# A gated linear-attention kernel: the key-value sums on two 64-column TensorE tiles, and an earlier load of the second x tile

## The chip, the cores and the metric

The kernel runs on one core of a Trainium2 chip. The metric is the device time of one execution in microseconds (us): 257.1 us before the change, the median of three runs (256.88 to 257.52). One profiled execution of the same kernel, from which every line of a profile below is taken, had a span of 255.7 us from its first to its last instruction.

The engines are TensorE (PE, matrix products; PEld is its loading of weights), VectorE (DVE), ScalarE (ACT), GpSimd (POOL) and SyncE (SP), whose queue issues most of the transfers. [...]

## What is computed

One block of 2048 tokens by 1024 features. Two branches share the input `x`, and a gate mixes them. Cut to what matters here:

```python
def reference(A_x, A_wqkv, A_wo, B_x, B_w_r, B_w_gate, B_w_up, B_w_down, gate_w):
    def _A_ref(x, wqkv, wo):
        B, S, D = x.shape
        H = 32; Dh = D // H                       # 32 heads of 32
        qkv = (x @ wqkv).reshape(B, S, 3, H, Dh).transpose(2, 0, 3, 1, 4)
        q, k, v = qkv[0], qkv[1], qkv[2]
        phi = lambda t: jnp.where(t > 0, t + 1, jnp.exp(t)) + 1e-6
        pq, pk = phi(q), phi(k)
        kv = jnp.einsum("bhsd,bhse->bhde", pk, v)  # 32 x 32 per head
        z = jnp.einsum("bhsd->bhd", pk)            # column sums of pk
        num = jnp.einsum("bhqd,bhde->bhqe", pq, kv)
        den = jnp.einsum("bhqd,bhd->bhq", pq, z)[..., None] + 1e-6
        return (num / den).transpose(0, 2, 1, 3).reshape(B, S, D) @ wo
    # _B_ref: one token, the one with the largest x @ w_r, gets a gated
    # feed-forward update; all others pass x through
    g = sigmoid((x * gate_w).sum(-1, keepdims=True))
    return g * a + (1 - g) * b
```

The part that changes is `kv` and `z`: a product over all 2048 tokens of the 32 columns of `pk` of a head with the 32 columns of `v` of the same head, and the sum of each `pk` column.

## The kernel before

The 2048 tokens are 16 tiles of 128. For each token tile, TensorE makes K and V (`unit_KV`; 8 matmuls for each 512 output columns), ScalarE and VectorE apply phi to K and write it to `pk`, and ScalarE copies V to `vt`. `unit_KVACC` then adds the tile's share to `kv`. It takes eight groups of 128 columns (four heads each). In each, `pk` is the stationary operand and `vt`, with a column of ones behind its 128 columns, the moving one. The result is 128 x 129: four useful 32 x 32 blocks on the diagonal, the products of different heads beside them, which nobody reads, and the column sums as column 128. The accumulators stay in three PSUM banks until the last token tile is done.

```python
def kv_slot(g):
    return kvacc[g // 3][:, 129 * (g % 3) : 129 * (g % 3) + 129]

def kv_open(t):
    if t not in pk_t:
        pk_t[t] = kvp.tile([P, D], BF, tag="pk", name=f"pk{t}")
        vt_t[t] = kvp.tile([P, NG, 129], BF, tag="vt", name=f"vt{t}")
        nc.gpsimd.memset(vt_t[t][:, :, 128:129], 1.0)

def unit_KVACC(t):
    for g in range(NG):
        pe.matmul(kv_slot(g), lhsT=pk_t[t][:, g * P : (g + 1) * P], rhs=vt_t[t][:, g, :],
                         start=False, stop=False, skip_group_check=True)
    del pk_t[t], vt_t[t]
```

The main loop puts this block of work between the K and V matmuls of the next token tile, beside the query matmuls (`unit_Q`) and pieces of the feed-forward branch (`ffn_step`; its matmuls use four 32-column tiles of TensorE side by side, as do the router logits `rps`, the denominators `dps` and the final sum `yps`):

```python
# ... rps: the router and gate logits of all tokens ...
for t in range(4):
    unit_KVACC(t)
for t in range(4, NT):
    for nb in range(4):
        unit_KV(t, nb)
        if nb == 1 and t > 4:
            unit_KVACC(t - 1)
        if (t, nb) in GU_AFTER:
            ffn_step(4)
        # ... steps of the down projection, on VectorE ...
    # ... unit_Q, once or twice per t; more ffn_step at the end of some t ...
unit_Q(*q_units.popleft())
unit_KVACC(NT - 1)
down_finish()          # yps
```

At the start, the first two token tiles of x are loaded as they are and transposed on TensorE (`unit_T`), and the rows of the K weights are used in the order in which they arrive:

```python
load_x(0, 1)           # all on SyncE's queue, in this order
load_k(0)
load_k(1)
load_x(1, 1)
for c in range(2, KC):
    load_k(c)
# ...
unit_T(0)
warm(3, 128)
first_mm(0, 0, 2)      # token tile 0, K rows 0 and 1
unit_T(1)
for c in range(2, KC):
    first_mm(0, c, c + 1)
    if c < KC - 1:
        first_mm(1, c - 2, c - 1)
first_mm(1, 5, 6)
es = [phi_exp(first[0][nb][:]) for nb in range(2)]
first_mm(1, 6, 8)
```

At the end, each token tile's output is made in two halves of 512 columns. The last half of the last token tile is cut in two, so that the last eviction and the last transfer are short.

Of the kernel before, what the change touches and what calls it, by code (L numbers as in the profile page):

```python
# [13 lines left out]
BF = mybir.dt.bfloat16  # L14
F32 = mybir.dt.float32
# [7 lines left out]
P = 128  # L23
# [3 lines left out]
NT = S // P  # L27
KC = D // P
NG = D // P
# [12 lines left out]
def kernel(  # L42
# [13 lines left out]
    nc = tc.nc  # L56
# [6 lines left out]
    keep = ctx.enter_context(tc.tile_pool(name="keep", bufs=1))  # L63
# [9 lines left out]
    def in_order(engine, names):  # L73
        last = [None]

        def wrap(fn):
            def call(*a, **k):
                inst = fn(*a, **k)  # L78
                if last[0] is not None and strict[0]:
                    tc.add_manual_dep(inst.ins, last[0].ins.name, NOSYNC, reason="program order on this engine")  # L80
                last[0] = inst
                return inst

            return call

        return SimpleNamespace(**{n: wrap(getattr(engine, n)) for n in names})

    pe = in_order(nc.tensor, ["matmul", "transpose"])
    dve = in_order(nc.vector, ["memset", "tensor_copy", "tensor_scalar", "tensor_scalar_add", "tensor_tensor", "scalar_tensor_tensor",
                               "reciprocal", "max", "max_index", "tensor_reduce", "stream_shuffle"])  # L90
    sp = in_order(nc.sync, ["dma_start", "dma_start_transpose"])
    act = in_order(nc.scalar, ["activation", "copy"])
# [1 line left out]
    pq_all = keep.tile([P, NG, S], BF)  # L94
    gate = keep.tile([P, NT], F32)
    omg = keep.tile([P, NT], F32)
    kvbd = keep.tile([P, NG, P], BF)
    zc = keep.tile([P, NG, 32], BF)
    mzc = keep.tile([P, NG, 32], F32)
    xp = dram.tile([S, D], BF, name="xp")  # L100
# [7 lines left out]
    kvp = ph1.enter_context(tc.tile_pool(name="kvp", bufs=4))  # L108
# [11 lines left out]
    def load_x(t0, n):  # L120
        xt4 = xin.tile([P, n, D], BF, name=f"xnat{t0}", bufs=1)
        sp.dma_start(out=xt4[:, 0:n, :], in_=x_v[:, t0 : t0 + n, :])
        for i in range(n):
            xnat[t0 + i] = xt4[:, i, :]

    def load_k(c):
        sp.dma_start(out=wkv[:, c, 0:D], in_=wqkv_v[:, c, D : 2 * D])

    load_x(0, 1)
    load_k(0)  # L130
    load_k(1)
    load_x(1, 1)
    for c in range(2, KC):
        load_k(c)
    for t in (2, 3):
        sp.dma_start_transpose(out=xT[:, :, t * P : (t + 1) * P], in_=x2d[t * P : (t + 1) * P, :])
# [37 lines left out]
    kvacc = []  # L174

    def kv_slot(g):
        return kvacc[g // 3][:, 129 * (g % 3) : 129 * (g % 3) + 129]

    def phi_exp(ps):
        u = tmp.tile([P, 512], F32, tag="phi_u")  # L180
# [5 lines left out]
    def phi_dve(ps, e0, out_ap):  # L186
        dve.scalar_tensor_tensor(out_ap, ps, EPS, e0[:], op0=ALU.max, op1=ALU.add)
# [11 lines left out]
    pk_t = {}  # L199
    vt_t = {}  # L200

    def kv_open(t):
        if t not in pk_t:
            pk_t[t] = kvp.tile([P, D], BF, tag="pk", name=f"pk{t}")
            vt_t[t] = kvp.tile([P, NG, 129], BF, tag="vt", name=f"vt{t}")
            nc.gpsimd.memset(vt_t[t][:, :, 128:129], 1.0)  # L206

    def kv_mm(ps, t, nb, c0, c1):
        for c in range(c0, c1):
# [3 lines left out]
    def kv_evac(ps, t, nb):  # L213
        if nb < 2:
            phi_dve(ps[:], phi_exp(ps[:]), pk_t[t][:, 512 * nb : 512 * nb + 512])
        else:
            act.copy(vt_t[t][:, 4 * (nb - 2) : 4 * (nb - 2) + 4, 0:128], ps[:].rearrange("p (g e) -> p g e", g=4))

    def unit_KV(t, nb):
        kv_open(t)  # L220
# [3 lines left out]

    def unit_KVACC(t):
        for g in range(NG):
            pe.matmul(kv_slot(g), lhsT=pk_t[t][:, g * P : (g + 1) * P], rhs=vt_t[t][:, g, :],
                             start=False, stop=False, skip_group_check=True)
        del pk_t[t], vt_t[t]

    def unit_Q(g, j):
        ps = ps_work.tile([P, 512], F32, tag="w")
        for c in range(KC):
            pe.matmul(ps[:], lhsT=wq[:, c, g * P : (g + 1) * P], rhs=xT[:, c, 512 * j : 512 * j + 512],
                             start=(c == 0), stop=(c == KC - 1))
        phi_evac(ps[:], pq_all[:, g, 512 * j : 512 * j + 512])
# [15 lines left out]
    def first_mm(t, c0, c1):  # L252
        for c in range(c0, c1):
            for nb in range(2):
                kv_mm(first[t][nb], t, nb, c, c + 1)

    unit_T(0)
    warm(3, 128)
    first_mm(0, 0, 2)
    unit_T(1)  # L260
    for c in range(2, KC):
        first_mm(0, c, c + 1)
        if c < KC - 1:
            first_mm(1, c - 2, c - 1)
    first_mm(1, 5, 6)
    es = [phi_exp(first[0][nb][:]) for nb in range(2)]
    first_mm(1, 6, 8)
    for nb in range(2):
# [3 lines left out]
    for t in (2, 3):  # L272
        kv_open(t)
        for nb in range(2):
            pool, tag = (ps_t, "t") if t == 2 else (ps_work, "w")
            ps = pool.tile([P, 512], F32, tag=tag)
# [1 line left out]
            kv_evac(ps, t, nb)  # L278
    ps_t_cm.__exit__(None, None, None)
    ps_acc = ph1.enter_context(tc.tile_pool(name="ps_acc", bufs=1, space=PSUM))  # L280
    kvacc += [ps_acc.tile([P, 512], F32, name=f"kvacc{i}") for i in range(3)]
    off16 = const.tile([P, 1], F32)
    dve.tensor_copy(off16[:], off16_i[:])
    for a in kvacc:
# [11 lines left out]
    for c in range(KC):  # L296
        for j in range(4):
            pe.matmul(rps[32 * j : 32 * j + 32, :], lhsT=wrg_pad[:, c, :], rhs=xT[:, c, 512 * j : 512 * j + 512],
                                  start=(c == 0), stop=(c == KC - 1), tile_position=(0, 32 * j))
# [219 lines left out]
    for t in range(4):  # L519
        unit_KVACC(t)  # L520
    for t in range(4, NT):
        for nb in range(4):
            unit_KV(t, nb)
            if nb == 1 and t > 4:
                unit_KVACC(t - 1)
            if (t, nb) in GU_AFTER:
                ffn_step(4)
            steps = DOWN_STEPS.get(t, ())
            if nb < len(steps):
                down_step(steps[nb])  # L530
        for i in range(Q_PER_T[t]):
            unit_Q(*q_units.popleft())
            if 4 + i < len(steps):
                down_step(steps[4 + i])
            if t == 4 and i == 0:
                router_part1()
                ffn_prefetch()
        if t == 5:
            router_part2()
        if (t, "end") in GU_AFTER:  # L540
            ffn_step(4)
    unit_Q(*q_units.popleft())
    unit_KVACC(NT - 1)
    down_finish()
    gates()
# [1 line left out]
    unit_Q(*q_units.popleft())  # L547

    zcol = keep.tile([P, NG], F32)
    for i in range(3):  # L550
        n = 3 if i < 2 else 2
        acc3 = kvacc[i][:, 0 : 129 * n].rearrange("p (g e) -> p g e", e=129)
        dve.tensor_copy(zcol[:, 3 * i : 3 * i + n], acc3[:, :, 128])
    dve.tensor_tensor(zc[:], mzc[:], zcol[:].unsqueeze(2).to_broadcast([P, NG, 32]), op=ALU.mult)
    for i in range(3):
        n = 3 if i < 2 else 2
        acc3 = kvacc[i][:, 0 : 129 * n].rearrange("p (g e) -> p g e", e=129)
        dve.tensor_copy(kvbd[:, 3 * i : 3 * i + n, :], acc3[:, :, 0:128])
    ph1.close()

    pb = ctx.enter_context(tc.tile_pool(name="pb", bufs=1))
# [51 lines left out]
    def unit_kvT():  # L613
        pt = four_banks("pt")
        for hf in range(2):
            for r in range(4):
                for c in range(4):
                    pe.matmul(pt[c][32 * r : 32 * r + 32, 32 * hf : 32 * hf + 32],
                              lhsT=kvbd[32 * c : 32 * c + 32, 4 * hf + r, 32 * c : 32 * c + 32],
                              rhs=ident[32 * c : 32 * c + 32, 32 * c : 32 * c + 32],  # L620
                              start=True, stop=True, tile_position=(32 * c, 32 * r))
        for c in range(4):
            eng = dve.tensor_copy if c % 2 else act.copy
            eng(kvT[:, :, c, :], pt[c][:, 0:64].rearrange("p (h d) -> p h d", h=2))
# [28 lines left out]
    for t in range(NT):  # L653
        xt = fin.tile([P, D], BF, tag="x3")
        nc.sync.dma_start(out=xt[:], in_=xp[t * P : (t + 1) * P, :])
        xg = fin.tile([P, D], F32, tag="xg3")
        strict[0] = True
        act.activation(xg[:], xt[:], ACTF.Copy, scale=omg[:, t : t + 1])
        strict[0] = False
        ot = fin.tile([P, D], BF, tag="o3")  # L660
        cols = [(0, 512), (512, 512)] if t < NT - 1 else [(0, 512), (512, 256), (768, 256)]
        for c0, cw in cols:
            ps = ps_work.tile([P, 512], F32, tag="w")
            for g in range(NG):
                pe.matmul(ps[:, 0:cw], lhsT=pq_all[:, g, t * P : (t + 1) * P], rhs=m_sb[:, g, c0 : c0 + cw],
                                 start=(g == 0), stop=(g == NG - 1))
            dve.scalar_tensor_tensor(ot[:, c0 : c0 + cw], ps[:, 0:cw], gate[:, t : t + 1],
                                           xg[:, c0 : c0 + cw], op0=ALU.mult, op1=ALU.add)
            if t == NT - 1:
                nc.sync.dma_start(out=out2d[t * P : (t + 1) * P, c0 : c0 + cw], in_=ot[:, c0 : c0 + cw])  # L670
        if t < NT - 1:
            nc.sync.dma_start(out=out2d[t * P : (t + 1) * P, :], in_=ot[:])
        if t == 0:
            rdB = den_group(1)
            normalise(rdB, 2)
            normalise(rdB, 3)
        norm_step(NORM_PER_T[t])
# [30 lines left out]
```

## The time and the profile before

| | value |
|---|---|
| time, median of 3 | 257.1 us (256.88 to 257.52) |
| span of the profiled execution | 255.7 us |
| busy: TensorE, VectorE, ScalarE, GpSimd | 97%, 58%, 49%, 18% |
| granted TensorE clock | 0.999 |
| K, V, Q and output matmuls of 512 columns, start to start | 0.216 us |
| 128 kv matmuls of 129 columns | 221 ns each as recorded |
| start of the first full-width K matmul; start of the unbroken stretch | 4.7 us; 8.4 us |
| last eviction | 483 ns, from 251.9 us |

How to read it. A matmul is recorded with its start and an end that is modelled. Matmuls follow each other much faster than the recorded length of one, so what a matmul costs the queue is the distance from its start to the next one's start. In the timeline, a line is a stretch of like instructions: start, length, engine, line of the program, operation, output and inputs, the part of the array in use (rows\*columns: 128\*32 is one of four column tiles), the shape, and how many. In brackets stands how long the engine was idle before and what ended that. The chain of waits goes back from the last instruction to what released each step, and gives the share of each engine in it.

### The profile page before, as it was taken

Reading aid. Unit: us, or ns where it says so; the run is one execution under the profiler, and the core shown is the slowest. Engines: PE = TensorE matmul, PEld = TensorE weight load, DVE = VectorE, ACT = ScalarE, POOL = GpSimd, SP = SyncE. Lnnn points to the kernel's source line nnn. Section 1 sums busy time; section 2 is a strip of 40 time slices with the busy share of each in tenths; the row PEclk is TensorE's granted clock in tenths of the full one; section 3 lists DMA queues with packets and bytes.
Section 4 is the critical chain, followed back from the end, with each engine's and each line's share of the span. In section 5 each row is a group of like instructions: output and inputs, shape, how many; then the busy total and the mean of one; then the engine's idle time right before and its main releaser. Section 6 shows DMA issues by size and latency. Waiting matters only on the chain.

```text
span 255.7 us, 3936 instructions
## 1 busy us (share of the span) xinstructions
PE 247.7 (97%) x1471; PEld 115.1 (45%) x1498; DVE 147.8 (58%) x243; ACT 125.7 (49%) x200; POOL 47.0 (18%) x94
## 2 busy tenths in 40 slices
PE   7899999999999999999999999999999999999993
PEld 3444455445444444445444444444444444444442
DVE  0046015232246349996799813584888999953442
ACT  2096334556354444645446445468889533333200
POOL 5000001010000000000000000210566779950000
PEclk9999999999999999999999999999999999999999
DMA  6999990009999999878897760030000474454122
GB/s 178 312 336 227 260 329 7 0 19 352 348 341 320 291 275 360 266 229 299 313 489 216 180 151 0 4 123 23 0 1 3 130 223 159 143 187 141 64 82 83
DMA packets 47498, 47.72 MB, mean 187 GB/s; under 512 B 18604, under 2 KB 35380, under 8 KB 47416
## 3 DMA queue, kind: packets, MB, share of 16 engines
q1 hardware_dynamic: 47192, 47.34, 60.6%
q8 instruction: 11, 0.18, 0.3%
q0 software_dynamic: 256, 0.14, 0.2%
q14 instruction: 7, 0.06, 0.1%
q10 hardware_dynamic: 32, 0.00, 0.0%
HBM read 39.34 MB, written 8.40 MB: 187 GB/s over the span
## 4 chain that ended last, share of the span: by engine, by line
PE 95%; DMA 2%; issue 1%; SPq 1%; DVE 0%
PE ps L78 86%; PE kvacc L78 3%; PE first L78 2%; DMA wkv<-in_A_wqkv_dram 2%; PE dps L78 1%; PE rps L78 1%; SPq L78 1%; PE pm L78 1%; PE yps L78 0%; DVE ot L78 0%; PE xs_ps L78 0%; PE hps L78 0%; PE pt L78 0%; PE wps L78 0%
## 5 line engine op out<-in xcount | busy, mean ns | idle before, releaser
L78 PE MATMUL ps<-wkv,xT 128*128 128x512 bf16 x465 | 107.1, 379 | 0.7
L78 PEld LDWEIGHTS <-xT 128*128 128x128 bf16 x512 | 48.8, 98 | 59.1 <-issue 4.5
L78 PE MATMUL ps<-xT,wq 128*128 128x512 bf16 x250 | 57.4, 379 | 0.6 <-issue 0.5
L78 ACT ACTIVATE u<-ps 128x512 f32<-128x512 f32 x60 | 35.9, 598 | 40.4 <-PE ps L78 37.2
L78 PE MATMUL ps<-m_sb,pq_all 128*128 128x512 bf16 (+1 forms) x259 | 55.3, 372 | 0.3
L78 ACT ACTIVATE e<-u 128x512 f32<-128x512 f32 x64 | 40.3, 630 | 2.0
L606 POOL TENSOR_TENSOR pq_all<-pq_all,rb 128x512 bf16<-128x512 bf16 x32 | 36.6, 1169 | 14.4 <-DVE rb L78 14.0
L78 PEld LDWEIGHTS <-pq_all 128*128 128x128 bf16 x264 | 25.8, 98 | 29.8 <-issue 0.4
L78 PEld LDWEIGHTS <-wq 128*128 128x128 bf16 x256 | 24.5, 98 | 30.3 <-issue 1.7
L78 DVE SCALAR_TENSOR_TENSOR pq_all<-ps,e 128x512 bf16<-128x512 f32 x32 | 22.0, 688 | 25.7 <-ACT e L78 25.6
L78 DVE SCALAR_TENSOR_TENSOR yacc<-wt,hcol,yacc 128x1024 f32<-128x1024 bf16 x27 | 34.6, 1281 | 2.2 <-DMA wt<-in_B_w_down_dram 1.7
L78 ACT CAST vt<-ps 128x512 bf16<-128x512 f32 x32 | 18.8, 588 | 34.5 <-PE ps L78 34.5
L78 DVE SCALAR_TENSOR_TENSOR ot<-ps,gate,xg 128x512 bf16<-128x512 f32 (+1 forms) x33 | 24.0, 735 | 15.0 <-PE ps L78 14.0
L78 ACT ACTIVATE xg<-xt,omg 128x1024 f32<-128x1024 bf16 x16 | 18.1, 1146 | 25.8 <-DVE ot L78 25.8
L78 DVE SCALAR_TENSOR_TENSOR pk<-ps,e 128x512 bf16<-128x512 f32 x28 | 19.2, 687 | 19.6 <-ACT e L78 19.6
L78 DVE STREAM_SHUFFLE rb<-rdp 128x512 f32<-128x512 f32 x32 | 22.8, 746 | 0.0
L206 POOL MEMSET vt<- 128x8 bf16 x16 | 1.9, 138 | 108.8 <-PE kvacc L78 108.8
L78 PEld LDWEIGHTS <-pk 128*128 128x128 bf16 x128 | 8.5, 98 | 3.3 <-issue 0.4
L78 PE MATMUL kvacc<-vt,pk 128*128 128x129 bf16 x128 | 9.7, 221 | 0.1
L78 PE MATMUL first<-wkv,xT 128*128 128x512 bf16 x31 | 7.8, 395 | 0.8 <-DMA wkv<-in_A_wqkv_dram 0.6
L78 DVE CAST r_bf<-rps 128x512 bf16<-128x512 f32 x1 | 0.7, 692 | 12.1 <-PE rps L78 12.1
L78 PE MATMUL ps<-wt,xs_pad 128*32 128x512 bf16 (+1 forms) x128 | 7.5, 355 | 0.0
(96 smaller groups left out, 78.6 us busy)
## 6 DMA issues: line engine op xcount, KB each, us to landing
wt<-in_B_w_down_dram SPq DMA_DIRECT2D x14, 512.0 KB, 5.5
wt<-in_B_w_gate_dram SPq DMA_DIRECT2D x8, 512.0 KB, 6.0
wt<-in_B_w_up_dram SPq DMA_DIRECT2D x8, 512.0 KB, 7.2
xt<-xp SPq DMA_DIRECT2D x16, 256.0 KB, 2.7
out_dram<-ot SPq DMA_DIRECT2D x15, 256.0 KB, 2.0
wt<-in_B_w_gate_dram SPq DMA_DIRECT2D x8, 384.0 KB, 5.7
wt<-in_B_w_up_dram SPq DMA_DIRECT2D x8, 384.0 KB, 6.5
wkv<-in_A_wqkv_dram SPq DMA_DIRECT2D x8, 256.0 KB, 5.6
```

The costliest lines, as they stand in the source:

```text
L78: inst = fn(*a, **k)
L206: nc.gpsimd.memset(vt_t[t][:, :, 128:129], 1.0)
L606: nc.gpsimd.tensor_tensor(sl, sl, rb[:], op=ALU.mult)
```

## The change

It has four parts.

- **Column tiles.** The stationary operand of a kv matmul is cut to 64 columns (two heads), and each half goes to one of two 64-column tiles of TensorE. The moving operand of each half is the 64 columns of V of the same two heads and a column of ones, 65 in all. Each result is 64 x 65, at PSUM partitions 0 to 63 or 64 to 127. This leaves out products of different heads that nobody reads. There are twice as many matmuls, each half as wide in both operands, and the intention is that the two of a pair run at the same time. The accumulators fit two banks instead of three, and the copy `kvbd` of them is half as wide.
- **Two token tiles per block.** Other matmuls use the whole array. The kv blocks of two token tiles are put one behind the other, so that the array changes its shape less often.
- **The start.** The second x tile is loaded ahead of K row 1, right behind K row 0, and its transposes go ahead of the matmuls with K row 1. The order of the first 32 K matmuls follows that.
- **The end.** The last half row of output is cut 384 + 128 instead of 256 + 256.

The core of the diff (cuts marked with `...`):

```diff
-    kvbd = keep.tile([P, NG, P], BF)
+    kvbd = keep.tile([P, NG, 64], BF)
...
     load_k(0)
-    load_k(1)
     load_x(1, 1)
-    for c in range(2, KC):
+    for c in range(1, KC):
         load_k(c)
...
-        return kvacc[g // 3][:, 129 * (g % 3) : 129 * (g % 3) + 129]
+        return kvacc[g // 4][:, 65 * (g % 4) : 65 * (g % 4) + 65]
...
-            vt_t[t] = kvp.tile([P, NG, 129], BF, tag="vt", name=f"vt{t}")
-            nc.gpsimd.memset(vt_t[t][:, :, 128:129], 1.0)
+            vt_t[t] = kvp.tile([P, NG, 2, 65], BF, tag="vt", name=f"vt{t}")
+            nc.gpsimd.memset(vt_t[t][:, :, :, 64:65], 1.0)
...
     def unit_KVACC(t):
         for g in range(NG):
-            pe.matmul(kv_slot(g), lhsT=pk_t[t][:, g * P : (g + 1) * P], rhs=vt_t[t][:, g, :],
-                             start=False, stop=False, skip_group_check=True)
+            for h in range(2):
+                pe.matmul(kv_slot(g)[64 * h : 64 * h + 64, :], lhsT=pk_t[t][:, g * P + 64 * h : g * P + 64 * h + 64],
+                          rhs=vt_t[t][:, g, h, :], start=False, stop=False, skip_group_check=True, tile_position=(0, 64 * h))
...
-    first_mm(0, 0, 2)
+    first_mm(0, 0, 1)
     unit_T(1)
-    for c in range(2, KC):
+    for c in range(1, KC):
         first_mm(0, c, c + 1)
         if c < KC - 1:
-            first_mm(1, c - 2, c - 1)
-    first_mm(1, 5, 6)
+            first_mm(1, c - 1, c)
...
-    kvacc += [ps_acc.tile([P, 512], F32, name=f"kvacc{i}") for i in range(3)]
+    kvacc += [ps_acc.tile([P, 512], F32, name=f"kvacc{i}") for i in range(2)]
...
-            if nb == 1 and t > 4:
+            if nb == 1 and t > 4 and t % 2 == 0:
+                unit_KVACC(t - 2)
                 unit_KVACC(t - 1)
...
     unit_Q(*q_units.popleft())
+    unit_KVACC(NT - 2)
     unit_KVACC(NT - 1)
...  # two copies of sums and of accumulators instead of three, and kvbd's new columns
-        cols = [(0, 512), (512, 512)] if t < NT - 1 else [(0, 512), (512, 256), (768, 256)]
+        cols = [(0, 512), (512, 512)] if t < NT - 1 else [(0, 512), (512, 384), (896, 128)]
```

More of the change, by code (lines that the diff above doesn't have):

```diff
@@ L216, in kv_evac @@
         else:
-            act.copy(vt_t[t][:, 4 * (nb - 2) : 4 * (nb - 2) + 4, 0:128], ps[:].rearrange("p (g e) -> p g e", g=4))
+            act.copy(vt_t[t][:, 4 * (nb - 2) : 4 * (nb - 2) + 4, :, 0:64], ps[:].rearrange("p (g h e) -> p g h e", g=4, h=2))
     def unit_KV(t, nb):
@@ L549 @@
     zcol = keep.tile([P, NG], F32)
[L550 to L553, printed above, removed]
+    for i in range(2):
+        acc4 = kvacc[i][:, 0:260].rearrange("p (g e) -> p g e", e=65)
+        dve.tensor_copy(zcol[:, 4 * i : 4 * i + 4], acc4[:, :, 64])
     dve.tensor_tensor(zc[:], mzc[:], zcol[:].unsqueeze(2).to_broadcast([P, NG, 32]), op=ALU.mult)
[L555 to L558, printed above, removed]
+    for i in range(2):
+        acc4 = kvacc[i][:, 0:260].rearrange("p (g e) -> p g e", e=65)
+        dve.tensor_copy(kvbd[:, 4 * i : 4 * i + 4, :], acc4[:, :, 0:64])
     ph1.close()
@@ L618, in unit_kvT @@
                     pe.matmul(pt[c][32 * r : 32 * r + 32, 32 * hf : 32 * hf + 32],
-                              lhsT=kvbd[32 * c : 32 * c + 32, 4 * hf + r, 32 * c : 32 * c + 32],
+                              lhsT=kvbd[32 * c : 32 * c + 32, 4 * hf + r, 32 * (c % 2) : 32 * (c % 2) + 32],
                               rhs=ident[32 * c : 32 * c + 32, 32 * c : 32 * c + 32],
```

## Prediction

> **What bounds the kernel now.** I read the page from the top: busy shares, the slices, then the chain that ended last. Four of its parts carry the case; in the slices one digit is a fortieth of the span, in tenths busy.
>
> ```profile
> PE 247.7 (97%) x1471; PEld 115.1 (45%) x1498; DVE 147.8 (58%) x243; ACT 125.7 (49%) x200; POOL 47.0 (18%) x94
> ...
> PE   7899999999999999999999999999999999999993
> ...
> PE 95%; DMA 2%; issue 1%; SPq 1%; DVE 0%
> ```
>
> TensorE (PE) is full from the second slice to the last but one, at full clock, and 95% of the chain is its own work. No other engine holds it anywhere between 8.4 us and 252 us. So the time is a sum over TensorE: what leaves that queue leaves the time. Only the first 8 us and the last 4 us have idle time of their own. A busy PE says nothing of how tightly its matmuls follow each other, so I take every cost below from distances between start times. The timeline of TensorE around one kv block (start, length, then the group):
>
> ```profile
> 52.76 0.38 PE L78 MATMUL ps<-wkv,xT 128*128 128x512 bf16 x1
> 52.98 0.64 PE L78 MATMUL kvacc<-vt,pk 128*128 128x129 bf16 x8
> 53.45 0.38 PE L78 MATMUL ps<-wkv,xT 128*128 128x512 bf16 x1
> ```
>
> Eight matmuls of 129 columns take 53.45 - 52.98 = 0.47 us of the queue, 59 ns each. In the trace the four-tile block starts at 37.27 and the next matmul at 39.17, which is 1.90 us for 32: the same 59 ns. All 128 come to 128 x 59 ns = 7.6 us, which the chain gives as 3% of the span. That is all that the kv part of the change can touch.
>
> The timeline of TensorE at the start:
>
> ```profile
> 4.70 1.06 PE L78 MATMUL first<-wkv,xT 128*128 128x512 bf16 x2
> 6.41 0.59 PE L78 MATMUL first<-wkv,xT 128*128 128x512 bf16 x2 [0.64 <-DMA wkv<-in_A_wqkv_dram]
> 7.68 0.62 PE L78 MATMUL pst<-ident,xnat 128*128 128x128 bf16 x8 [0.68 <-DMA xnat<-in_A_x_dram]
> 8.36 6.20 PE L78 MATMUL first<-wkv,xT 128*128 128x512 bf16 x27
> 14.40 0.38 PE L78 MATMUL ps<-wkv,xT 128*128 128x512 bf16 x1
> ```
>
> Each group starts when a transfer lands: K row 1 at 6.4, the second x tile at 7.7, K row 2 at 8.3. From 8.36 nothing waits: 28 matmuls at 0.2157 us (one record is missing) end at 14.40.
>
> [...] The timeline round one visit to 32-column tiles:
>
> ```profile
> 67.72 0.59 PE L78 MATMUL ps<-xT,wq 128*128 128x512 bf16 x2
> 68.24 1.05 PE L78 MATMUL ps<-wt,xs_pad 128*32 128x512 bf16 x16
> 69.22 0.39 PE L78 MATMUL ps<-wkv,xT 128*128 128x512 bf16 x1
> ```
>
> Two full matmuls from 67.72 would hand over at 68.15; the tiles start at 68.24, 0.09 later. Their four rounds of four end at 68.24 + 4 x 0.2157 = 69.10; the next starts at 69.22, 0.12 later. So a visit costs 0.21 us, about 0.10 us per change of mode. Four 32-column tiles with four different moving operands took only one matmul's time per round, so column tiles really do run together here.
>
> [...] No run here has a 64-column load. What the trace has is the tight end of full-width loads, in the timeline of the four-column matmuls:
>
> ```profile
> 92.41 0.24 PE L78 MATMUL hps<-sel,h_bf 128*128 128x4 bf16 x4
> 92.52 0.38 PE L78 MATMUL ps<-wkv,xT 128*128 128x512 bf16 x1
> ```
>
> Four pairs of load and matmul in 0.11 us are at most 27 ns each, with a 128-column load in each. [...]
>
> **The change part by part.** *Removed*: 128 matmuls of 129 columns, 7.6 us. *Added*: 128 pairs of 65-column matmuls, the two of a pair on the two column tiles. The floor of a pair is its streaming: 65/129 of 59 ns, or 30 ns. The weights of the next pair can load behind the matmul, as 32-column loads do now, but the load must fit. [...] 128 x 37 = 4.7 us.
>
> *Added*: changes of mode. In the program order of the changed kernel there are seven kv blocks. Four (tiles 4-5, 8-9, 10-11 and 12-13) stand between full matmuls: two changes each, 8. The other three have 32-column work on one side already (the router logits ahead of tiles 0-3, the gate/up tiles behind tiles 6-7, the reduction of y behind tiles 14-15): one more change each, 3. Eleven changes x 0.103 us = 1.1 us. With the blocks of before (13, all but the first of one token tile) there would be six more to enter and leave. The sum of the kv part is 4.7 + 1.1 - 7.6 = -1.8 us, all of it on the path.
>
> *Moved*: the second x tile takes the place of K row 1 in the queue; both are 256 KB. The x tile should land near 6.4 us and row 1 near 7.65. The transposes then run in the hole before row 1. From 7.67 the order is row 1 for tile 0, row 0 for tile 1, row 2, and so on, 30 matmuls without a wait: a row is used every 4 x 0.2157 = 0.86 us, while the trace has rows 2 to 7 landing at 8.31, 8.95, 9.63, 10.30, 10.95 and 11.76, ahead of the uses at 8.5, 9.4, ... 12.8. So this stage ends at 7.67 + 30 x 0.2157 = 14.14 instead of 14.40: -0.26 us. Tile 0 is finished after 26 matmuls instead of 22, at 13.28 instead of 13.10, which starts ScalarE's chain 0.2 us later; the banks it frees are wanted first at 17.6, over 2 us after they come free, so that costs nothing.
>
> *The end*: the last half row is cut 384 + 128 instead of 256 + 256. Timeline of the last piece:
>
> ```profile
> 250.70 1.15 PE L78 MATMUL ps<-m_sb,pq_all 128*128 128x256 bf16 x9
> 250.81 0.75 PEld L78 LDWEIGHTS <-pq_all 128*128 128x128 bf16 x7
> 250.97 1.75 SPq L670 DMA_DIRECT2D out_dram<-ot  x3
> 251.88 0.48 DVE L78 SCALAR_TENSOR_TENSOR ot<-ps,gate,xg 128x256 bf16<-128x256 f32 x1 [0.39 <-PE ps L78]
> ```
>
> VectorE's eviction took 752 ns at 512 columns and 484 at 256, so about 216 + 1.05 per column: 618 ns at 384 and 350 at 128. TensorE's stream ends at about 251.68 either way. The 384-column eviction can start 0.45 us before that plus the 0.2 us from the matmul to VectorE, and ends at +0.37; the small one then runs to about +0.74. Now it is +0.69. I put the end at +0.05 us: the smaller last eviction is given back by waiting for the larger one ahead of it.
>
> *Off the path*: two bank clears and two pairs of copies instead of three, on VectorE; 16 instead of 8 ones columns on POOL. Nothing waits for them (the sums for the denominator are ready at 164.4 us and used at 166.3). The gate/up weights land at least 2.2 us before their use in the trace, so TensorE being 1 us early meets no wait.
>
> Sum: 257.1 - 1.8 - 0.26 + 0.05 = 255.1; I say 255.3, for loads that show at the head of each block and waits I have not seen.
>
> **Rivals.** [...] *The tiles overlap perfectly*: 30 ns a pair, 3.8 us, and 254.3. For it: the 32-column tiles of one round start 3 to 4 ns apart. *The two tiles do not overlap* and queue: 60 ns a pair, and the 1.1 us of mode changes come on top, near 258.2. Those same rounds speak against it. *The start gains nothing* because tile 1's data land later than row 1 did: then 0.26 us is missing.
>
> **Range and chances.** The pair decides: 30 to 45 ns spans 254.3 to 256.2, and that is where I put three quarters; the slow load gets most of the rest. Hence 254.1 to 257.5. Two per cent is 5.1 us; the whole kv work is 7.6 us, so faster by that would need pairs at about 13 ns, and slower pairs near 90 ns. Both chances are small.
>
> **What would show it.** In the changed profile: a two-tile kv block of 32 matmuls should take about 16 x 37 = 0.6 us plus 0.2 us for coming and going, against 2 x 0.47 now; start distances show the pair. The transposes of the second x tile should start at 6.4 and the first `ps` matmul at 14.1. The last VectorE eviction should follow the one before without a gap. The prediction is wrong if pairs take over 50 ns, if a change of mode costs other than 0.1 us, or if TensorE shows new waits for weights or for pk and vt.

## The result

The changed kernel takes 254.23 us (median of four runs, 254.06 to 255.78) where the kernel before takes 257.21 beside it. The ratio is 0.9898, with a 95% interval of 0.9857 to 0.9939: about 2.6 us less, between 1.6 and 3.7. The predicted time was 255.3; the measured one lies just inside the predicted range of 254.1 to 257.5.

The page of the changed kernel, the lines that answer to those of before (busy shares, TensorE in the slices, the chain by engine):

```profile
PE 246.5 (98%) x1626; PEld 110.6 (44%) x1626; DVE 146.4 (58%) x240; ACT 125.4 (50%) x200; POOL 47.6 (19%) x94
...
PE   7999999999999999999999999999999999999993
...
PE 95%; DMA 2%; SPq 0%; DVE 0%; issue 0%; DVEq 0%
```

The picture is the same: TensorE full, 95% of the chain on it. The waits of TensorE in the changed kernel are 1.0 us for the first instruction and 0.5 and 0.6 us for the first transfers, no other. So nothing new holds it, and its queue got shorter. The number of recorded matmuls tells nothing here: a few of before were missing from the record.

The timeline of TensorE in the changed kernel, one kv block of two token tiles, and below it the start:

```profile
60.01 0.59 PE L78 MATMUL ps<-wkv,xT 128*128 128x512 bf16 x2
60.54 0.70 PE L78 MATMUL kvacc<-vt,pk 128*64 128x65 bf16 x32
61.17 0.39 PE L78 MATMUL ps<-wkv,xT 128*128 128x512 bf16 x1
```

```profile
4.78 0.60 PE L78 MATMUL first<-wkv,xT 128*128 128x512 bf16 x2
5.91 0.62 PE L78 MATMUL pst<-ident,xnat 128*128 128x128 bf16 x8 [0.53 <-DMA xnat<-in_A_x_dram]
7.09 6.63 PE L78 MATMUL first<-wkv,xT 128*128 128x512 bf16 x30 [0.56 <-DMA wkv<-in_A_wqkv_dram]
13.56 1.24 PE L78 MATMUL ps<-wkv,xT 128*128 128x512 bf16 x5
```

The block holds the queue from 60.54 to 61.17, 0.63 us for two token tiles (2 x 0.47 before), plus 0.09 us ahead of it: two full matmuls from 60.01 would hand over at 60.44. Inside the block the start times in the trace come in pairs, 3 to 6 ns apart. The second pair starts 52 ns after the first; from there on one pair comes every 31.8 ns.

The start falls from 14.40 to 13.56 us for the first `ps` matmul, 0.83 us, where 0.26 was expected. For everything behind the start I use one distance throughout, from the first `ps` matmul to the first matmul of the sum of y (`yps`): it holds all kv blocks, and TensorE doesn't wait in it. Its last line in the timeline of before, and below it in that of the changed kernel:

```profile
162.09 0.42 PE L78 MATMUL yps<-yacc,ones_f 128*32 128x256 f32 x4
```

```profile
159.06 0.41 PE L78 MATMUL yps<-yacc,ones_f 128*32 128x256 f32 x2
```

The distance is 147.69 us before and 145.50 us after, so the kv part is worth **2.20 us**. Together with 0.83 at the start and 0.04 given back at the end, that is the 2.99 us between the two spans (255.70 and 252.72).

### The profile page after: what moved, and what is told of

The parts are those of the page before. It is cut to its first block, busy times and chain, and to the rows that moved or that the text cites. A ratio compares the mean times of both kernels' runs of the same rounds, so it can differ in the third digit from the quotient of the medians.

```text
span 252.7 us, 4218 instructions
## 1 busy us (share of the span) xinstructions
PE 246.5 (98%) x1626; PEld 110.6 (44%) x1626; DVE 146.4 (58%) x240; ACT 125.4 (50%) x200; POOL 47.6 (19%) x94
## 4 chain that ended last, share of the span: by engine, by line
PE 95%; DMA 2%; SPq 0%; DVE 0%; issue 0%; DVEq 0%
PE ps L78 88%; PE first L78 3%; PE kvacc L78 2%; DMA wkv<-in_A_wqkv_dram 2%; PE dps L78 1%; PE rps L78 1%; PE pm L78 1%; SPq L78 0%; DVE ot L78 0%; PE yps L78 0%; PE xs_ps L78 0%; DVEq L702 0%; PE pt L78 0%; PE hps L78 0%; PE wps L78 0%
## 5 line engine op out<-in xcount | busy, mean ns | idle before, releaser
L78 PE MATMUL ps<-xT,wq 128*128 128x512 bf16 x256 | 58.4, 379 | 0.0
L78 PE MATMUL ps<-m_sb,pq_all 128*128 128x512 bf16 (+2 forms) x264 | 55.6, 373 | 0.0
L78 DVE SCALAR_TENSOR_TENSOR ot<-ps,gate,xg 128x512 bf16<-128x512 f32 (+2 forms) x33 | 23.8, 733 | 15.1 <-PE ps L78 14.2
L205 POOL MEMSET vt<- 128x16 bf16 x16 | 2.5, 191 | 105.5 <-PE kvacc L78 105.0
L78 PE MATMUL first<-wkv,xT 128*128 128x512 bf16 x32 | 7.2, 379 | 0.7 <-DMA wkv<-in_A_wqkv_dram 0.6
L78 DVE SCALAR_TENSOR_TENSOR pk<-first,e 128x512 bf16<-128x512 f32 x4 | 2.8, 691 | 8.6 <-ACT e L78 8.6
L514 POOL DMA_DIRECT2D xp<-brow x1 | 0.6, 573 | 34.3 <-DVE zcol L78 34.3
```

Of the source, the lines that this page charges most:

```text
L205: nc.gpsimd.memset(vt_t[t][:, :, :, 64:65], 1.0)
L514: nc.gpsimd.dma_start(out=xp[bass.ds(nonlocal_idx[0], 1), :].rearrange("o (j n) -> (o j) n", j=4), in_=brow[0:128:32, :])
```

## Experiments

The theory: the two 64-column tiles run side by side at the pace of a weight load or a stream (about 32 ns a pair), and each change of the array's shape costs about 0.11 us. The rivals: the gain is owed to the start, the changes of shape are free, or narrow matmuls are cheap on any tile. Twelve kernels ran, two of them (`before_look` and `moving33`) once each, so that only their traces are read. The ratios are to the kernel before, run beside each; "distance" is the one defined above.

### The parts alone

`start_only`: the kernel before with the new order of loads and of the first K matmuls, and nothing else.

```diff
     load_k(0)
-    load_k(1)
     load_x(1, 1)
-    for c in range(2, KC):
+    for c in range(1, KC):
         load_k(c)
# and the order of first_mm as in the change
```

> The kernel before with nothing but the new start: second x tile loaded behind K row 0, K matmuls in the new order. Theory A (the order itself brings the second x tile and K row 1 half a microsecond earlier): transposes of tile 1 near 5.9 us, the unbroken K matmuls from 7.1, first ps matmul near 13.6, and 0.8 us off the time of before. Theory B (the landings of the profiled run of the changed kernel were a chance of that run): row 1 near 7.6, first ps matmul near 14.1, 0.3 us off the time. Either way the kv blocks stay at 59 ns a matmul.

Ratio 0.9982 (0.9970 to 0.9994): 0.46 us less, between 0.15 and 0.77. The kv blocks stay at 59 ns a matmul, and the distance is 147.70. The timeline of TensorE in this run:

```profile
6.38 0.62 PE L78 MATMUL pst<-ident,xnat 128*128 128x128 bf16 x8 [0.54 <-DMA xnat<-in_A_x_dram]
7.53 6.63 PE L78 MATMUL first<-wkv,xT 128*128 128x512 bf16 x30 [0.52 <-DMA wkv<-in_A_wqkv_dram]
14.00 0.38 PE L78 MATMUL ps<-wkv,xT 128*128 128x512 bf16 x1
```

The same order, but the tile is here at 6.4, as predicted, and not at 5.9. That speaks for theory B.

`kv_only`: the changed kernel with the old start and the old end.

```diff
-    load_x(1, 1)
-    for c in range(1, KC):
+    load_k(1)
+    load_x(1, 1)
+    for c in range(2, KC):
         load_k(c)
# first_mm as before; the last half row 256 + 256
```

> The changed kernel with the old start and the old end: only the 64-column tiles and the two-tile blocks. If the parts add up, 2.2 us off the time of before, first ps matmul again at 14.4 us, kv blocks of 0.63 us for two token tiles. Rival (the kv part only uncovers another wait, and the gain is owed to the start): under 1 us off.

Ratio 0.9911 (0.9886 to 0.9937): 2.3 us less, between 1.6 and 2.9. The distance is 145.50, to 0.01 us that of the changed kernel, and two-tile blocks take 0.63 us. The rival falls: the gain is the kv part's. The first `ps` matmul missed what I wrote. It came at 13.47 us, with the *old* order.

`before_look`: the kernel before once more, unchanged (a comment line at its end), for its start.

```diff
+# a second look
```

> The kernel before once more, for a second look at its start. If the landings move from run to run by themselves, the first ps matmul comes somewhere between 13.4 and 14.5 us and not again at 14.40; if they are fixed by the order of the queue, at 14.4.

```profile
6.18 0.59 PE L78 MATMUL first<-wkv,xT 128*128 128x512 bf16 x2 [0.74 <-DMA wkv<-in_A_wqkv_dram]
6.84 0.62 PE L78 MATMUL pst<-ident,xnat 128*128 128x128 bf16 x8
7.60 6.20 PE L78 MATMUL first<-wkv,xT 128*128 128x512 bf16 x27
13.64 0.81 PE L78 MATMUL ps<-wkv,xT 128*128 128x512 bf16 x3
```

The same kernel started its `ps` matmuls at 14.40 in one run and at 13.64 in another; the distance is 147.69 in both. So the landings of the first transfers move by themselves, by over half a microsecond. Of the 0.83 us between the two first profiles, the order accounts for about 0.25 (the fourth landing is waited for and not the fifth, 0.68 us apart in the trace of before, and two more matmuls, 0.43 us, follow it). The other 0.6 is less than the 0.76 us by which the start of one and the same kernel moved here, so I put it down to chance. Eleven runs with the new order gave 13.08 to 14.00, 13.44 in the mean; three with the old 13.47 to 14.40, 13.83 in the mean. What makes the landings move was not looked for.

`end_old`: the changed kernel with the last half row 256 + 256.

```diff
-[(0, 512), (512, 384), (896, 128)]
+[(0, 512), (512, 256), (768, 256)]
```

> The changed kernel with the last half row cut 256 + 256 as before. From the evictions that the traces show (616 ns at 384 columns, 340 at 128, 484 at 256): the stream of TensorE ends at the same time, the last transfer is issued 0.08 us earlier than in the changed kernel, and the time is the same within 0.1 us. Rival (the small last transfer was worth something): 0.2 us slower or more.

Ratio 0.9901 (0.9877 to 0.9925), not to be told from the changed kernel. From the end of the last stream to the end of the span the traces have 4.07 us with 384 + 128, and 4.03 with 256 + 256.

### Changes of shape

`one_tile_blocks`: one token tile per block again, 13 blocks and 22 changes of shape for 7 and 11.

```diff
-            if nb == 1 and t > 4 and t % 2 == 0:
-                unit_KVACC(t - 2)
+            if nb == 1 and t > 4:
                 unit_KVACC(t - 1)
...
-    unit_KVACC(NT - 2)
     unit_KVACC(NT - 1)
```

> The changed kernel with one token tile per kv block, as before: 13 blocks in place of 7, so 22 changes of the array's shape in place of 11. If a change costs 0.10 to 0.13 us, 1.1 to 1.4 us slower than the changed kernel, that is about 255.5 us; a single block 0.38 us from its first matmul to the next full one. Rival (the changes are free, hidden in the matmuls' own latency): no difference.

Ratio 0.9956 (0.9942 to 0.9970), 255.39 us. The distance is 146.74, 1.24 us more, which is 0.113 us for each of the eleven changes. Its timeline has a single block:

```profile
94.57 0.59 PE L78 MATMUL ps<-wkv,xT 128*128 128x512 bf16 x2
95.09 0.45 PE L78 MATMUL kvacc<-vt,pk 128*64 128x65 bf16 x16
95.47 0.39 PE L78 MATMUL ps<-wkv,xT 128*128 128x512 bf16 x1
```

From 95.00 (94.57 and two full matmuls) to 95.47 is 0.47 us for one token tile: what the full-width block took. With single blocks that stand between full matmuls the tiles gain nothing; all that they save goes into two changes of shape. There the grouping is what makes them pay. This kernel's distance is still 0.95 us shorter than before's: by the start times 0.75 us come from the four-tile block behind the router logits and about 0.1 us from each of the three blocks beside 32-column work; the other nine lose about 0.01 us each.

`placed`: four blocks (tiles 0-3, 4-6, 7-10, 11-15), each beside 32-column work, and a fifth buffer for `pk` and `vt`.

```diff
-kvp = ph1.enter_context(tc.tile_pool(name="kvp", bufs=4))
+kvp = ph1.enter_context(tc.tile_pool(name="kvp", bufs=5))
...
-            if nb == 1 and t > 4 and t % 2 == 0:
-                unit_KVACC(t - 2)
-                unit_KVACC(t - 1)
+            if (t, nb) == (7, 1):             # ahead of ffn_step
+                for tt in range(4, 7):
+                    unit_KVACC(tt)
...
+        if t == 11:                           # ahead of ffn_step
+            for tt in range(7, 11):
+                unit_KVACC(tt)
...
-    unit_KVACC(NT - 2)
-    unit_KVACC(NT - 1)
+    for tt in range(11, NT):
+        unit_KVACC(tt)
```

> The changed kernel with four kv blocks in place of seven (token tiles 0-3, 4-6, 7-10, 11-15), each beside matmuls on 32-column tiles, with a fifth buffer for pk and vt. Four changes of the array's shape in place of eleven. At 0.117 us each, as the one-tile blocks gave, 0.8 us faster than the changed kernel; the 31.8 ns a pair stays. Rival (longer blocks delay what reads pk and vt buffers, and waits come up in their place): no gain.

Ratio 0.9868 (0.9842 to 0.9895). The distance is 144.72: 0.78 us less for seven changes, 0.112 us each (the 0.117 in the expectation should have been the 0.113 above). No wait came up in their place.

### The pair

`halves_apart`: all eight matmuls of one column tile, then the eight of the other.

```diff
-        for g in range(NG):
-            for h in range(2):
+        for h in range(2):
+            for g in range(NG):
```

> The changed kernel with the loop over the halves outside: the eight matmuls of one column tile, then the eight of the other. Theory (the gain comes from two neighbours in the queue running on different tiles at the same time): each of the 16 matmuls of a token tile then takes the 30 ns of its own stream, 0.48 us in place of 0.25, which is 3.7 us over the kernel: about 258 us. Rival (a 65-column matmul takes 16 ns of the queue anyway, whichever tile it is on): no difference.

The distance is 147.09, 1.59 us more than in the changed kernel and not 3.7; ratio 0.9958 (0.9940 to 0.9977). A two-token-tile block in its timeline:

```profile
59.85 0.59 PE L78 MATMUL ps<-wkv,xT 128*128 128x512 bf16 x2
60.38 0.91 PE L78 MATMUL kvacc<-vt,pk 128*64 128x65 bf16 x32
61.22 0.39 PE L78 MATMUL ps<-wkv,xT 128*128 128x512 bf16 x1
```

0.84 us in place of 0.63. The start times within the block suggest why it lies between the two expectations. The first five matmuls start alone, the second 53 ns after the first and the others 29 to 36 ns apart: that is how neighbours on one tile follow each other here, near the 30 ns of the theory, and the rival (16 ns on any tile) falls. Then a start comes 6 ns behind another, and further on 0 to 7 ns, closer than any two of those five. The trace does not name the tile of a matmul. I infer that the sixth start is the other half's first matmul, three places ahead of its turn; so the halves overlapped in part.

`moving33`: 33 moving columns in place of 65, weights of 64 columns. It leaves out half of the products, and the sums.

```diff
-kv_slot(g)[64 * h : 64 * h + 64, :]  ...  rhs=vt_t[t][:, g, h, :]
+kv_slot(g)[64 * h : 64 * h + 64, 0:33]  ...  rhs=vt_t[t][:, g, h, 0:33]
```

> The changed kernel with the moving operand of each kv matmul cut from 65 to 33 columns, weights of 64 columns as before. This leaves out half of the products and the sums. If the 31.8 ns of a pair are the stream of 65 columns, a pair falls to the 25 ns that the shortest matmuls show, or to 17 ns if loads allow. If the load of 64 columns sets them, a pair stays at 30 ns or more.

```profile
59.65 0.81 PE L78 MATMUL ps<-wkv,xT 128*128 128x512 bf16 x3
60.39 0.69 PE L78 MATMUL kvacc<-vt,pk 128*64 128x33 bf16 x32
61.01 0.82 PE L78 MATMUL ps<-wkv,xT 128*128 128x512 bf16 x3
```

The block takes 0.62 us in place of 0.63, and by the start times a pair still takes 31.6 ns. Halving the stream changes almost nothing, so the stream of 65 columns does not set the pace of a pair. What is left, as an inference, is the load of 64 columns: behind loads of 32 columns the same 33-column streams came in groups of four, a group every 25 ns, for the first 32 matmuls of a block (`tiles32`, below). No run changes the load alone.

### Four tiles, and the best of both

`tiles32`: four 32-column tiles with 33 moving columns each, blocks as in the changed kernel.

```diff
-            for h in range(2):
-                pe.matmul(kv_slot(g)[64 * h : 64 * h + 64, :], lhsT=pk_t[t][:, g * P + 64 * h : g * P + 64 * h + 64],
-                          rhs=vt_t[t][:, g, h, :], ..., tile_position=(0, 64 * h))
+            for h in range(4):
+                pe.matmul(kv_slot(g)[32 * h : 32 * h + 32, :], lhsT=pk_t[t][:, g * P + 32 * h : g * P + 32 * h + 32],
+                          rhs=vt_t[t][:, g, h, :], ..., tile_position=(0, 32 * h))
# vt [P, NG, 4, 33], one PSUM bank of accumulators, kvbd [P, NG, 32]
```

> The changed kernel with four 32-column tiles and 33 columns in place of two of 64 and 65; two-token-tile blocks stay where they were. If the stream alone sets the pace, a group of 128 columns takes 17 ns in place of 32: 1.9 us less, and three changes of shape fall away (the neighbours have the same shape): 2.2 us faster than the changed kernel. If a load and its matmul can't follow each other on a tile in less than the 25 ns that the four-column matmuls show, 25 ns: 1.2 us faster. If 512 more instructions cost queue time: no gain.

Ratio 0.9905 (0.9882 to 0.9927); the distance is 145.38, only 0.12 us less than with 64-column tiles. That is close to the third expectation, "no gain", though its reason (the number of instructions) is not shown. The timeline of a block, now 64 matmuls:

```profile
59.67 0.81 PE L78 MATMUL ps<-wkv,xT 128*128 128x512 bf16 x3
60.41 0.68 PE L78 MATMUL kvacc<-vt,pk 128*32 128x33 bf16 x64
61.03 0.39 PE L78 MATMUL ps<-wkv,xT 128*128 128x512 bf16 x1
```

The block takes 0.61 us (61.028 - 60.415 in the trace). Its first 32 matmuls start in groups of four, a group every 25 ns after the first, as the second expectation has it. From there to the end of the block they start about 8.4 ns apart, one by one: 33 to 37 ns for four, slower than the 64-column pair. Three changes of shape did fall away: the 32-column matmuls behind a block start 0.01 us after its last one, and the first block starts 0.21 us after the last router matmul. At 0.112 us each that is 0.34 us, of which the slower matmuls took back all but 0.12.

`tiles32_placed`: 32-column tiles in the four placed blocks (both diffs above).

> Both: 32-column tiles, and the four blocks beside 32-column work, so that no kv block changes the array's shape by itself. The two gains should add: 1.3 us for eleven changes, 0.9 to 1.9 us for the groups, so 2.2 to 3.2 us faster than the changed kernel, near 251.5 us on a chip where before takes 257.

Ratio 0.9880 (0.9855 to 0.9905). The distance is 144.49, 1.01 us less than in the changed kernel and not 2.2 or more: behind their first 28 to 32 matmuls the long blocks run at about 8.4 ns a matmul.

`best64` and `best32`: the placed blocks with 64- and with 32-column tiles, the new start, the old end (diffs above).

> The four placed blocks of 64-column tiles, the new start, and the old end of 256 + 256. 0.8 us from the blocks and 0.04 us from the end: a ratio near 0.987 to before, 0.3% under the changed kernel.

> The same with 32-column tiles. The traces of the last runs put it 0.2 us ahead of the 64-column form from the first ps matmul to the sum of y, since its four blocks cost no change of shape but its matmuls come only every 8.3 ns once the first thirty are gone. A ratio near 0.986; the two can hardly be told apart.

Ratios 0.9868 (0.9844 to 0.9893) and 0.9856 (0.9831 to 0.9880), with distances 144.71 and 144.49. Both beat the kernel before by 1.3 to 1.4%. By the traces they are 0.8 and 1.0 us ahead of the changed kernel behind the start; the intervals of the ratios overlap with its own, and with each other.

## Why the prediction was right, point by point

- **The bound.** Right: a sum over TensorE's queue. In each experiment with a ratio, the change of distance with 0.25 us for the new start and 0.04 us for the new end lies in the interval of the time, and in the changed kernel TensorE waits for nothing but its first instruction (1.0 us) and the first transfers (0.5 and 0.6 us).
- **The pair, 37 ns.** This is the term that was mis-sized. No run shows it: it was my estimate, 7 ns over the 30 ns that I had worked out for the stream. The pair measured 31.8 ns, about 2 ns over those 30: 4.1 us for 128 pairs in place of 4.7. The pairing held: the two of a pair start 3 to 6 ns apart, and `halves_apart`, which gives up part of that, loses 1.59 us. The stream of 65 columns is not what sets the pace (31.6 ns with 33 columns in `moving33`), which leaves the load, as an inference.
- **The changes of shape, 11 x 0.103 = 1.1 us.** Measured 0.112 to 0.113 each by adding eleven and by taking seven away, 1.2 us for eleven. These two runs give the price of a change in this kernel, whatever it is made of.
- **The sum of the kv part, -1.8 us.** Measured -2.20: 0.6 less for the pairs, 0.1 more for the changes, the rest rounding and the heads of blocks.
- **The start, -0.26 us.** About right for the order: 0.25 us by the landings of the trace of before, 0.46 us by the clock in `start_only`, with an interval (0.15 to 0.77) that holds 0.26. It need not be so much in every run: with the old order `kv_only` reached its `ps` matmuls at 13.47, ahead of the changed kernel. The absolute landings I took from one profile (6.4 and 7.65 us) were the weak part: 5.9 and 7.05 in the changed kernel's profile, and moving from run to run with the order fixed. The later start of ScalarE's chain cost nothing, as said: from the first `ps` matmul to the router logits are 21.03 us in both kernels.
- **The end, +0.05 us.** Measured +0.04, but not for the reason given. The small last eviction wasn't held up as far as I had it: it started at 248.94, while the larger one was still recorded until 249.02, and ended 0.63 us after the stream in place of the predicted 0.74. It is SyncE's queue that comes late. It issues the two transfers 0.43 us apart, the last one 0.82 us after the stream (0.71 before). The timeline of the last piece of the changed kernel, where SPq has three transfers in 1.92 us and DVE both evictions in one line:

```profile
247.94 1.92 SPq L669 DMA_DIRECT2D out_dram<-ot  x3
248.40 0.87 DVE L78 SCALAR_TENSOR_TENSOR ot<-ps,gate,xg 128x384 bf16<-128x384 f32 x2 [0.49 <-PE ps L78]
```

- **The time.** I had 1.8 us off (257.1 to 255.3), and the medians of the result are 2.98 us apart. Of the 1.2 us between the two, by the traces, 0.4 us are the kv part and 0.6 us the part of the start that the order does not explain; the last 0.2 us are what I had added for heads and waits. So half of the miss I put down to chance, and about 2.4 us is what the change itself is worth (2.20 + 0.25 - 0.04).
- **The rivals.** A slow load, to which the chances gave most of what lies outside 30 to 45 ns a pair, shows in no run: the pair measured 31.8 ns. The two tiles in turn at 60 ns fell too; the perfect overlap at 30 ns was nearer than my own number.

## What to carry to other kernels

When one engine's queue is the whole span, cost a change by start-to-start distances in that queue, and count what surrounds the new work too: here a visit to another tile shape costs 0.22 us, which for one token tile is all that the narrower matmuls save. Group such work, and put it beside work of the same or of an already different shape. Take transfer landings from several profiles before a prediction rests on half a microsecond of them.

## What the hardware showed that I had not expected

- With 32-column tiles (`tiles32`), matmuls of 33 columns ran four at a time every 25 ns only for the first 32 of a block (28 in the one behind the router logits), and then one every 8.4 ns or so. No run shows the cause.
- In `halves_apart`, by the spacing of the start times, a matmul of the second column tile seems to have begun while three of the first tile, ahead of it in the program, had not started: the sixth start comes 6 ns behind the fifth. That is an inference, and it fails if two matmuls of one tile can start 0 to 7 ns apart, which they do nowhere at the head of these blocks (29 to 53 ns).
- A full-width matmul of 129 columns cost 59 ns here, and a pair of 64 x 65 cost 32 ns for the same useful output. By itself that is a gain of 3.5 us in this kernel; the changes of shape took 1.2 of it.
